# Residual codec kernel: output stores issued by ScalarE's queue, loads alone on SyncE's, and all queues ordered anew

## The chip, the core and the metric

The kernel runs on one core of a Trainium2 chip. The metric is device time in microseconds. Times before come from three runs (615.65, 626.93 and 618.35 us); one further execution was profiled.

## The reference

A sequence x of 2 x 16000 rows of 512 channels (bfloat16) is filtered along time with three taps per channel, put through SiLU, quantized by four residual stages of eight code vectors each, and the sum of the chosen vectors is filtered with three taps again:

```python
for i in range(K):                      # K = 3
    z = z + xp[:, i:i+T, :] * dw_enc[i][None, None, :]
z = _silu(z)
res = z
for s in range(Nq):                     # Nq = 4, eight vectors in each codebook
    cb = codebooks[s]
    d2 = |res|^2 - 2.0 * res @ cb.T + |cb|^2
    idx = d2.argmin(-1)
    sel = cb[idx]
    q = q + sel
    res = res - sel
for i in range(K):
    y = y + qp[:, i:i+T, :] * dw_dec[i][None, None, :]
```

(The line of d2 is shortened; xp and qp are z's input and q padded by one row at both ends.)

## The kernel before

The rows are cut into 18 tiles. A tile has G groups of 128 rows; 14 tiles have G = 16, and the first and last two have 6 and 8. Partition p of a tile holds the G consecutive rows that begin at its row G*p, and neighbouring tiles overlap by two rows, for the filters.

The steps of one tile, with the lines that the profile names:

- **Load.** G transposing DMAs from SyncE, one a group (L557), and one each for the rows before and behind (L565, L571), write the channels onto partitions in XT. There are two XT buffers.
- **Taps, SiLU.** For each half of the channels: three multiplications on VectorE or ScalarE (L599, L598), two sums on VectorE (L386), the exponential on ScalarE (L604), plus one (L606 or L605), the reciprocal on ScalarE (L616), the product on VectorE (L386, ZB). The exponential and the reciprocal need different tables, which ScalarE loads in between (1.28 us each).
- **Decide.** Products of ZB with itself and the codebooks on TensorE (L635), evacuated by VectorE (L669, L670); three stages of small VectorE instructions choose a vector and set a one-hot row; TensorE and a copy (OT, L716 on ScalarE or L717 on VectorE) turn it round for the next stage's correction. POOL copies one-hot rows (L704, L707).
- **Residual.** TensorE subtracts the chosen vectors from ZB in PSUM (L793, L798), eight evacuations a tile write ZB back (L820 on ScalarE or L821 on VectorE), and a fourth decision follows (L836 to L846).
- **Back.** TensorE applies the decoder to windows of one-hot rows (L762, then L870); each product of 1024 columns is cast from PSUM into half of a YB buffer, on ScalarE (L879) or VectorE (L880). There are four YB buffers of four groups each.
- **Store.** When both halves of a YB are written, SyncE issues its store (L902), from the same queue as the loads. The rows that overlap with a neighbouring tile are left out, and a store is cut so that most of it covers a multiple of 16 partitions. So one step issues one to three transfers: 128 partitions at once, or 112, 15 and 1. There are 64 such steps and 130 transfers.

All steps are entered into a list with their dependences and a planned duration, and a planner (class Plan, L17 to L182) hands out the order. Two strings of constants fix it: RANK, a rank for each step, by which each engine's queue is sorted; and WHERE, one letter for each step that can run on either of two engines (A for ScalarE, D for VectorE). The planned durations matter at one place: the planner lays the queues out in time, emits the instructions of all engines in the order of their planned starts, and puts filler products on TensorE (L922) where it expects TensorE to wait for over 1 us. Each engine then executes its own instructions strictly in that order. Transfers take turns on eight completion lanes in the order in which they are emitted, whichever engine issues them, and each waits until the previous one on its lane has landed.

In the store step before, the planned duration is 0.5 us on SyncE ("SP") with a tail of 4.0 us until the data has landed; a load is planned at 1.36 us (1.56 us in the first two tiles) with a tail of 1.5 us.

Of the kernel before, what the change touches and what calls it, by code (L numbers as in the profile page):

```python
# [12 lines left out]
ACT = mybir.ActivationFunctionType  # L13
# [172 lines left out]
def kernel(  # L186
# [32 lines left out]
    RANK = ("000102010102060500040d0h050a0d0V00090E010d0q0u070v0a0j0c0p030t0f0B020j0e0f0g0i0l0m0n0r0306080b0k0o0p0q03040e00050a06080c"  # L219
            "04060b05070103090d020h0p0z0n0m07070C0D0L0M0P0R0U0j0q0t040v0g0z0h0f15171l13161c040g0i0Z1f1g0b080900080605090x0A0F0G0c0J0K"  # L220
            "0O0W0f0g0i0r0h0l0i020n0H0o0S0y0N0s0k0l10190e0m0r0w0c0T0e0Y0a0I0b0Q0k110j0X120o14180u1k1d0s1a1b1e1h1i1j0w1r0y1t0A1w0k0l1A"
            "1B1C1D1E1F1G0s0m1J0n1K1L1M1N1O1P1Q1R1S1T0t0o1V0p1W1X1Y1Z202122230u0q250r0s0I270t0v0K0L0w0y0Q0M0z0A0P0O0C0D2o2r2t2x2D0F0V"
            "0J2S0K0X1A0N2Y1d09080d0e0b0c070f030a1o1m1n0x1p1s1q1u0C0E0B1x1v1y1z1H0D1I0F1U0G240H260u0x2b2e2f2g2h2i2j0v0B2m0E2k2p2s2y2u"
            "2z2B2C2E2F0w0G0U0H2G2H2I2L2M2N2O2P0x0I2R0L0M0Y0Z0O0P11140Q0R13120S0T15160U0V37383a3c3d0Y1a121l131n1P111c141h1q0w0m0k0x0g"
            "0u0j0l0h0v0s0i0r0q0p0t0n0o292a0J282c0N2d2l0S2Q2n2q2v0R2w0T2A2K0W2T103117390W0X3g0Z103j3l3n3q3s3v3x0y151f163z3C3D3F3B3E3H"
            "3I3J3K0z171j183M3O3Q3P3R3S3T3U0C1b1m1d1e1q1p1g1h1s1t1i1j1v1u1k1l1x1y1o1p4q1r1t4K4O4P4R4T1H1O1N1S1P1Y271O1R1Q1U251M1T1X1X"
            "2h1V1W1W202c0M0A0I0P0O0C0K0D0G0y0L0z0H0F0B0E0N0J2X2W2U2V2Z303233191b351834363b3e3f3i1d3t1e3N1g3L191c3Z1a1f41454447494b4d"
            "0A1m4f1n4i4l4o4r4j4m4s4t4u4v0B1q4z1s4w4x4y4B4C4E4F4G0G1u1C1w1x1E1G1z1C1I1J1D1E1K1L1F1G1M1N1J1K5e1S1U5t5v5x5y5B1Y5H262327"
            "252m252222242l2j2j2p2l2s2i2g2r2n2w1513110W120V0Y0R0X0Q0S0T170Z0U1014163m3o3k3p3r3u3w3y1k3Y1i3G3A3V3W1o3X401w4k1z4A1A4D1v"
            "1y4S1A1B4U4W4V4X4Z502J520D1I1P1L555a5c5f5d5g5h5j5k5m0E1R5r1T5o5p5q5u5w5z5A5C0K205K2829282b2a2b272a2d2f2d2e2g2h2f2h2l2q6t"  # L230
# [29 lines left out]
    WHERE = ("ADDADADADDDADDDDDDDDADAAAAAAADADDDDADDAADDDDADDADAAAAAAAAAAAAADDADADDDDDAADDAAAAAAAAAAAAAAAAAAAADDDDDDADADDDDDDDAAAAAAAA"  # L260
            "ADAAAAAAAADDDDDDDADDDADDADDAAAAAAAADAAADAAAADDDADDDDDDDADDADDDAAAAAAAAAAAAAAAADDADDDDDDDDDDDDADAAAAAAAADAAAAAAAADDDDDDDD"
            "DDDDDDAADAADAAAAAAAAAAAAAADDDDDDDDADDADDDAAAADAAADAAAAAAAAAADDDDDDDDDDDDDDAADAAAAAADAAAAAAAAAADDDDDDDDDDDDDDDDDDAAAAAAAA"
            "AAAAAAAADDDADDDDDDDDDDDDDADAAAAAAAAAAAAAAADDDDDDDDDDDDADAAAAAAADAAADAAAAAAAADDADDDDDDDDDDDDDDAAAADAAADAAADAAAADDDDDDDDDD"
            "DDDDADDADAAAAAAAAAAAAAADDDDDDDDDDDDDDDADDADAAADDADAAAADDAADDDDDDDDDDDDDDADDAAAAAAADDAAADDDDDDDADADDDDDDDAAADDADADDAAD")
# [286 lines left out]
    def load(st):  # L551
# [6 lines left out]
        for g in range(G):  # L558
            add("SP", 1.56 if n < 2 else 1.36, ("load", n, 0.01 * g), lambda g=g: one(g), [], [("X", n % NX, g + 1)], tail=1.5)
# [3 lines left out]
        if t0 and n:  # L563
            before = xf[r0 - 1:r0 - 1 + G * P, :].rearrange("(p g) d -> g p d", g=G)[0]
            add("SP", 1.56 if n < 2 else 1.36, ("load", n, 0.01 * G), lambda: nc.sync.dma_start_transpose(out=X[:, :, 0, :], in_=before), [], xe, tail=1.5)  # L565
# [286 lines left out]
    def back(st):  # L852
        n, GH = st["n"], st["GH"]
        W = OHW[n % NW]
        for k0 in range(0, GH, 2):
# [5 lines left out]
            for k in ks:  # L861
# [98 lines left out]
```

## Time and profile before

| What | us |
|---|---|
| Median of three runs (lowest, highest) | 618.35 (615.65, 626.93) |
| The profiled execution, whole time | 618.01 |
| The profiled execution, its span | 616.2 |
| TensorE busy | 512.9 |
| POOL busy | 57.3 |

The span reaches from the first to the last instruction of the profiled execution. SPq and ACTq are the DMA issues of SyncE and ScalarE; the profile doesn't count them as busy time of an engine. The granted clock of TensorE was 0.971 of full speed on the mean. The DMA engines moved 72.1 MB at a mean of 117 GB/s, and the transfers of SyncE's queue took 54.0% of the sixteen DMA engines' time.

### The profile page before, as it was taken

What the parts mean: (1) busy time and instruction counts of PE and PEld (TensorE: products, weight loads), DVE (VectorE), ACT (ScalarE), POOL (GpSimd) and SP (SyncE); (2) the same over time, 40 slices, a digit from 0 to 9 for tenths busy, and PEclk for the clock granted to TensorE, in tenths of its full rate; (3) what the DMA queues carried; (4) which work ended last, traced back from release to release, by engine and by line L of the source; (5) the groups of instructions that cost most, each with busy time, mean ns of one, the idle gap of its engine ahead of it and who ended that gap; (6) DMA issues with size and microseconds to landing.
All of it is one profiled execution on the core that took longest, in us unless ns stands there. A gap on an engine that the chain in (4) does not pass through costs nothing.

```text
span 616.2 us, 27776 instructions
## 1 busy us (share of the span) xinstructions
PE 512.9 (83%) x12628; PEld 241.8 (39%) x12628; DVE 557.3 (90%) x1110; ACT 548.9 (89%) x432; POOL 57.3 (9%) x93
## 2 busy tenths in 40 slices
PE   4979879788967777888877888869987889989994
PEld 1435334244434233343442343433344244434542
DVE  6887998999999999999998999979999999997653
ACT  2895889989999999999988999879998999999764
POOL 3000000301010010202010000100012011110000
PEclk9898979999998999999997999989999999999998
DMA  5455555556558935575665657566664734602336
GB/s 114 82 99 92 100 88 88 111 114 115 103 97 140 172 80 122 87 168 121 115 171 74 171 114 166 105 121 140 131 129 84 171 99 103 157 4 105 107 118 203
DMA packets 163981, 72.10 MB, mean 117 GB/s; under 512 B 155568, under 2 KB 155600, under 8 KB 163863
## 3 DMA queue, kind: packets, MB, share of 16 engines
q1 hardware_dynamic: 163646, 69.90, 54.0%
q8 instruction: 98, 1.61, 1.1%
q10 hardware_dynamic: 216, 0.43, 0.3%
q14 instruction: 21, 0.16, 0.2%
HBM read 0.43 MB, written 32.77 MB: 54 GB/s over the span
## 4 chain that ended last, share of the span: by engine, by line
ACT 29%; DVE 28%; PE 13%; SPq 12%; issue 11%; DMA 6%; DVEq 0%; ACTq 0%
SPq L557 10%; ACT YB L879 7%; DVE ZB L386 7%; ACT ZB L820 6%; ACT EX L616 5%; ACT EX L604 5%; DMA XT<-in_x_dram 4%; DVE TB L599 4%; DVE TA L386 3%; PE banks L870 3%; PE banks L793 3%; PE banks L635 3%; DVE EX L606 2%; DVE TA L599 2%; PE banks L798 2%
## 5 line engine op out<-in xcount | busy, mean ns | idle before, releaser
L879 ACT CAST YB<-banks 128x1024 bf16<-128x1024 f32 x117 | 113.6, 1029 | 14.0 <-DMA out_dram<-YB 4.5
L820 ACT CAST ZB<-banks 128x1024 bf16<-128x1024 f32 (+2 forms) x125 | 108.9, 926 | 14.6 <-PE banks L798 14.3
L604 ACT ACTIVATE EX<-ZB 128x4096 bf16<-128x4096 bf16 (+2 forms) x36 | 115.1, 3196 | 5.3 <-DVE ZB L386 5.2
L922 PE MATMUL banks<-MSK,IDENT 128*128 128x512 bf16 x465 | 115.1, 389 | 2.3 <-DVE S L670 0.7
L616 ACT ACTIVATE EX<-EX 128x4096 bf16<-128x4096 bf16 (+2 forms) x36 | 115.0, 3199 | 0.2
L635 PE MATMUL banks<-ZB 128*32 128x64 bf16 x8064 | 92.0, 198 | 5.7 <-issue 3.0
L635 PEld LDWEIGHTS <-ZB 128*32 128x32 bf16 x8064 | 77.1, 96 | 48.9 <-issue 43.6
L599 DVE TENSOR_SCALAR TB<-XT,WENC 128x2048 bf16<-128x2048 bf16 (+2 forms) x128 | 86.8, 689 | 7.3 <-DMA XT<-in_x_dram 3.6
L870 PE MATMUL banks<-WDEC,OHW 128*128 128x512 bf16 x252 | 75.3, 389 | 21.6 <-ACT YB L879 11.4
L798 PE MATMUL banks<-OHR,WR 32*128 32x512 bf16 (+2 forms) x1152 | 82.0, 357 | 0.9 <-ACT OHR L750 0.8
L707 POOL COPY OHD<-OHA 128x256 bf16<-128x256 bf16 (+2 forms) x36 | 36.3, 1007 | 461.8 <-DVE OHA L386 461.8
L386 DVE TENSOR_TENSOR TA<-TA,TB 128x4096 bf16<-128x4096 bf16 (+2 forms) x36 | 72.7, 2018 | 4.8 <-ACT TB L598 3.7
L386 DVE TENSOR_TENSOR ZB<-ZB,EX 128x4096 bf16<-128x4096 bf16 (+2 forms) x36 | 73.2, 2036 | 2.9 <-ACT EX L616 2.9
L386 DVE TENSOR_TENSOR ZB<-TA,TB 128x4096 bf16<-128x4096 bf16 (+2 forms) x36 | 72.9, 2026 | 0.9 <-ACT TB L598 0.8
L793 PE MATMUL banks<-ZB,IDENT 64*64 64x512 bf16 (+2 forms) x576 | 55.0, 370 | 13.2 <-ACT YB L879 3.6
L922 PEld LDWEIGHTS <-IDENT 128*128 128x128 bf16 x465 | 42.5, 99 | 50.6 <-issue 8.4
L793 PE MATMUL banks<-ZB,UP 64*64 64x512 bf16 (+2 forms) x576 | 52.9, 354 | 0.0
L599 DVE TENSOR_SCALAR TA<-XT,WENC 128x2048 bf16<-128x2048 bf16 (+2 forms) x65 | 44.6, 695 | 5.5 <-DMA XT<-in_x_dram 4.4
L798 PEld LDWEIGHTS <-WR 32*128 32x128 bf16 x1152 | 23.7, 93 | 59.4 <-issue 51.2
L793 PE MATMUL banks<-ZB,DOWN 64*64 64x512 bf16 (+2 forms) x576 | 41.9, 367 | 0.0
L870 PEld LDWEIGHTS <-OHW 128*128 128x128 bf16 x252 | 20.7, 98 | 45.2 <-issue 25.2
L606 DVE TENSOR_SCALAR EX<-EX 128x4096 bf16<-128x4096 bf16 (+2 forms) x33 | 36.7, 1112 | 1.3 <-ACT EX L604 1.3
(129 smaller groups left out, 566.8 us busy)
## 6 DMA issues: line engine op xcount, KB each, us to landing
out_dram<-YB SPq DMA_DIRECT2D x33, 448.0 KB
out_dram<-YB SPq DMA_DIRECT2D x28, 512.0 KB
XT<-in_x_dram SPq DMA_TRANSPOSE x283
out_dram<-YB SPq DMA_DIRECT2D x30, 60.0 KB
out_dram<-YB SPq DMA_DIRECT2D x31, 2.0 KB
out_dram<-YB SPq DMA_DIRECT2D x2, 224.0 KB
YB<-in_dw_dec_dram ACTq DMA_DIRECT2D x1, 384.0 KB
out_dram<-YB SPq DMA_DIRECT2D x1, 384.0 KB
```

Source lines behind the costliest of these rows:

```text
L386: add("DVE", cost, key, lambda: nc.vector.tensor_tensor(out=out, in0=a, in1=b, op=op), reads, writes, **kw)
L557: nc.sync.dma_start_transpose(out=X[:, :, g + 1, :], in_=src[g])
L599: lambda dst=dst, src=src, w=w: nc.vector.tensor_scalar(out=dst, in0=src, scalar1=w, scalar2=None, op0=ALU.mult),
L604: add("ACT", act(2 * R), ("exp", n, h), lambda: nc.scalar.activation(v(ex), Z, ACT.Exp, scale=-1.0), zt, [("EX", sl), "ACTTAB"], hold="E")
L616: nc.scalar.add_instruction(mybir.InstActivation(name=nc.get_next_instruction_name(), engine=mybir.EngineType.Activation, func=ACT.Reciprocal,
L635: nc.tensor.matmul(o[HB * q:HB * (q + 1), u * ZW:(u + 1) * ZW].rearrange("p (s c) -> p s c", s=2), lhsT=blk, rhs=both, start=False, stop=( ...
L793: nc.tensor.matmul(at(r)[to], lhsT=dia[h, h], rhs=Z[h, i, r:G:RG, :], start=start, stop=False)
L798: nc.tensor.matmul(at(r), lhsT=WR[v][g, i * P:(i + 1) * P], rhs=W[g, v // 3, 0:rows_of[r], :], start=False, stop=stop)
L820: either({"ACT": act_psum(2 * k * P), "DVE": dve(2 * k * P)}, key(1), lambda dst=dst, src=src: nc.scalar.copy(dst, src()), lambda dst=dst, ...
L870: nc.tensor.matmul(o, lhsT=W[:, k, PADC:PADC + P], rhs=WDEC[u], start=True, stop=not wrap)
L879: either({"ACT": act_psum(1024), "DVE": dve(1024)}, key, lambda dst=dst, box=box: nc.scalar.copy(dst, ps(box)), lambda dst=dst, box=box: n ...
L922: nc.tensor.matmul(PS[j // 2][:, 512 * (j % 2):512 * (j % 2) + NMK * ZW], lhsT=IDENT, rhs=MSK.rearrange("p u w -> p (u w)"), start=True, s ...
```

## The change

The store step is entered for ScalarE in place of SyncE, and its transfers are issued by ScalarE's queue. Its planned duration is now 0.06 us and 0.1 us for each of its transfers; the cutting of the store into transfers (pieces) is taken out of the old function, unchanged, to count them. Loads stay on SyncE, planned at 1.4 in place of 1.36 us. RANK and WHERE are both replaced as a whole, so every queue has a new order, and some steps change between ScalarE and VectorE. Nothing else differs: the steps, their sizes and their number are the same.

```diff
-    RANK = ("000102010102060500040d0h050a0d0V00090E010d0q0u070v0a0j0c0p030t0f0B020j0e0f0g0i0l0m0n0r0306080b0k0o0p0q03040e00050a06080c"
...
+    RANK = ("00010200040706000203090b060d0b0P02070o0i0s0608010r0y0J0c0v0h0F0w0z0i0s050c0h0k0l0m0o0p0307080f0g0j0n0u00050k05030d01040h"
...
-    WHERE = ("ADDADADADDDADDDDDDDDADAAAAAAAADADDDDADDAADDDDADDADAAAAAAAAAAAAADDADADDDDDAADDAAAAAAAAAAAAAAAAAAAADDDDDDADADDDDDDDAAAAAAAA"
...
+    WHERE = ("DAADDDDDADADDDDAAADDAAAAAAAAADADADDDDDAADDDDDDDDDAAAAAAAAAAAAADDADADDDDADDADDAAAAAAAAAAAAAAADAAAADDDDDDADADDDDDDDAAAAAAA"
...
         for g in range(G):
-            add("SP", 1.56 if n < 2 else 1.36, ("load", n, 0.01 * g), lambda g=g: one(g), [], [("X", n % NX, g + 1)], tail=1.5)
+            add("SP", 1.56 if n < 2 else 1.4, ("load", n, 0.01 * g), lambda g=g: one(g), [], [("X", n % NX, g + 1)], tail=1.5)
...
-            add("SP", 0.5, ("back", n, ks[-1] / GH), lambda Y=Y, g0=2 * k0, g1=2 * (ks[-1] + 1): store(st, Y, g0, g1), [("Y", y)], [],
+            parts = pieces(st, 2 * k0, 2 * (ks[-1] + 1))
+            add("ACT", 0.06 + 0.1 * len(parts), ("back", n, ks[-1] / GH), lambda Y=Y, g0=2 * k0, parts=parts: store(st, Y, g0, parts), [("Y", y)], [],
                 tail=4.0)
 
-    def store(st, Y, g0, g1):
-        r0, a, e, G = st["row0"], st["a"], st["e"], st["G"]
-        view = outf[r0:r0 + G * P, :].rearrange("(p g) d -> p g d", g=G)
+    def pieces(st, g0, g1):
+        a, e, G = st["a"], st["e"], st["G"]
         runs = []
...
-        for p0, p1, lo, hi in split:
-            nc.sync.dma_start(out=view[p0:p1, lo:hi, :], in_=Y[p0:p1, lo - g0:hi - g0, :])
+        return split
+
+    def store(st, Y, g0, parts):
+        r0, G = st["row0"], st["G"]
+        view = outf[r0:r0 + G * P, :].rearrange("(p g) d -> p g d", g=G)
+        for p0, p1, lo, hi in parts:
+            nc.scalar.dma_start(out=view[p0:p1, lo:hi, :], in_=Y[p0:p1, lo - g0:hi - g0, :])
```

The two loads of the neighbouring rows (L565, L571) change as L559 does.

More of the change, by code (lines that the diff above doesn't have):

```diff
@@ L260 @@
[L260 to L264, printed above, removed]
+    RANK = ("00010200040706000203090b060d0b0P02070o0i0s0608010r0y0J0c0v0h0F0w0z0i0s050c0h0k0l0m0o0p0307080f0g0j0n0u00050k05030d01040h"
+            "030708040a0206090c0c0b0o0C0p0l01060t0B0K0L0N0R0X0i0i0u0a0v0d050h0j14161l111b1c0p0e0e0Y121f0b08090g0q0l04040a0C0G0H0e0O0Q"
+            "0S0T0f0f0j0n0e02000f0m0M0A0D0j0I0903190g0m0k0u0n0x0d0U0g0Z070E0a0W0V10151317180q1a0s1n0r1e1g1d1h1i0t1j0w0y0z1v0A1x0k0l1B"
+            "1D1C1E1F1G1H0q0m0F0n1I1J1L1N1M1O1P1Q1R1S0r0o1X0p1T1U1V1Y1Z2021220t0q240r0s0K0J0u0w0N0M0x0y0S0O0z0A0R0Q0C0D2p2s2u2w2x0F0W"
+            "0J2R0L0Y110N2X150f0c0a080e09010d0b050x1o1k1m1p1q1r1s0D0E0B1t1u1w1y1z1A1K0G1W0H230I250t0v292b2c2e2f2g2h0v0B2k0E2i2j2t2v2o"
+            "2r2z2B2D2E0w0G2H0H2G2J2L2K2M2N2O2P0x0I2Q0K0M0Z100O0P17130Q0R14160S0T19180U0V3638393a3c0Y1d121j151o1r101g131l1w0o0r0v0j0u"
+            "0p0x0l0q0n0t0k0s0g0w0i0m0h27280L262a0P2d2l0U2F2q0T2n2m2y0V2C2I0X2S122Z1a370W0X3e0Z113i3k3j3m3p3r3t0y141i163x3B3D3E3z3C3F"
+            "3G3I3J0z171n183L3O3Q3P3R3S3T3U0C1b1q1d1e1u1t1f1h1x1y1i1j1z1D1k1l1C1B1o1p4u1s1t4L4O4Q4S4T1H1S1K1W1Q1Y211N1X1O5s241P1V1X23"
+            "261T201W22290H0A0E0J0F0L0B0G0N0O0M0y0I0P0C0z0K0D2V2T2U2W2Y3130321c1e351b33343b3f3d3g1f3u1h3M1k3K191c3X1a1g40444346484a4c"
+            "0A1m4k1n4e4h4j4l4n4p4q4r4s4t0B1q4x1r4v4w4z4A4B4C4D4F0D1v4H1w1x1I1M1z1A1L1N1D1E1Q1P1F1G1R1T1L1M5i1R1U5t5v5x5z5B1Y5F282b22"
+            "2c2h2528272a2j2k2q2m2r2u2i2p2j2t2w170Z0U100R0W0Q0X0V16120T1514110Y130S3q3n3l3o3s3w3v3y1p3Y1m3H3N3A3V1s3W3Z1A4g1E4y1F4E1u"
+            "1y4M1B1C4V4Y4X4Z50512A530E1I571J55595d5f5a5c5g5h5j5l0F1S5r1V5o5q5u5w5y5A5C5E0L205K26292e5Z2a2b2f2i2c2f2l2m2g2h2n2o2l2r6w"
+            "2s2t6D6H6I6K6M2B6O2E2E2I2G2I2D2D2F6T2L2J2H2M2J2Q2O2M2Q2N2P1c1l1n1d1b1j18191m1o1e1a1f1k1g1h1p1i4142451v47494b4d1G4J4o4i4m"
+            "4f4G1H4I4K1J4U1U5m1Z5D21235L1Z245O5S5Q5V5W5X3h610G2d2g2e6365696b686c6e6f6h6j0J2o6l2p6m6n6q6s6t6v6y6A0P2u6C2v2w6J2y2x2z2A"
+            "2B2C2R7k2O2S2T2U2S2W2X7D33357I7K7P7R7T39343c383j3e3m3b373e393b3f3a3g3c3k3i3d3n3i3p1x1G1D1y1u1w1E1v1q1A1r1C1F1z1t1s1H1B4P"
+            "4R1K4N4W521O54255M565b585e5k5p5n5G275T2d642k6g2n2q6x2y2A6Q6W6V6X6Z70710M2K742P7375777b797c7e7g7i7l0O2U2T2V7o7q7s7r7t7u7v"
+            "7w0Q2Y7y2Z302Z2Y32363132373833353m3o3g3h3s3v8t3y3A8G8K8N8Q8S3F8W3L3x3K3z3C3P3A3R3E3J3Q3B3T3D3G3M3y3S3I3L1M1L1N1V1Z1U1W1Y"
+            "1P1X1I1Q1J1S1T1O1K1R5J5N5I5H5P5U5R5Y2s6z676066626a6i6d6k2v6G2x6L2z6R2G2H6Y2L2N767h7d7j7z7B7E0R312X347G7M7O7Q7J7N7S7U7W7Y"
+            "0S3a363d80838584878b8d8e0T3p8i3r3t3l3q3u3w8A3o3B3C3s3t3D3E3v3u3H3I913N3O95999d9i9k443S483W4c40424d3Y4i414d493V4g3Z4e4F4i"
+            "4H4l4m2g28292e2a2c23252421272b2f2022262d0H0I6o6u6p6r6B6F6E6N2F7a6U2C6S6P722K787f2V7A2W7H30813h3k883l3q8j8n8m8o8q8r8u0U3x"
+            "8y3z8x8z8B8D8C8E8H8J8M8R0V3G8Y3J8T8V8X909296989b0W3V3F3X3Y3K3M3Z409n3O41423Q3P43469w3U4a4b9G4e4j9T9W9Ya0a24m444q464pak4c"
+            "4J4o4N4q4t4M4p4Q4v4z4P4s4W4w4R2u2m2x2i2k2t2l2s2n2o2q2w2p2v2r2j0K0N2h2R7n7m7p7x7F7C7L3f8l7Z7X827V868a898c3j8v3n8F3r8Z3U3W"
+            "9e45479v9B9z9D9F9H9I0X4f9K4h9L9P9S9V9O9U9X9Za1a30Y4na54oa6a8aaa9abacaeaf104sah4u4v48494w4x4b4a4y4z4f4k4A4Bay4h4L4OaO4S4U"
+            "b3b5b7b9bb4Y4x5b4I5c4J4U5j4N5o4Q4W5p4S5r4V4X5y515x53552P2D2L2E2A2z2N2G2M2y2I2C2K2F2O2H2J2B8g8h8f8k8p8s8w8I3w948O8U8P8L93"
+            "9a979c3N9t3R9A3T9E4k4lad4r4tajapalaratavax0Z4D4j4IaBaDaEaGaFaHaJaLaNaP114RaT4TaUaXaZaYb1b2b4b6144Vbd4Z51bq4B52534A4C5557"
+            "4E4G58594H4F5d5fbL5q5sc0c2c4c6c85C545H575F595b5P5d5T5g5i5M5a5N5c5f5R5e5S5h5j302V372T2U2W31342R2X2Y353236332Q2Z2S9g9f9h3H"
+            "9j9m9l9o3X9N9p9q9s9r9u9x9y9C43ag45an47as4C4Eaz4G4KaIaVaQb0b8babc124Xbf50bebgbibkbjblbmbnbobp1354bs56bvbybzbxbBbCbEbG165a"
+            "bJ5e5g4LbO5h5i4O4M5k5l4TbT5t5u4Z4Y5z5Bck5A5EcqctcvcycA5J585V5k6a5x5I695y6i5A5H685w6f5C5M665u6e5B5N3p3m3k3g3o3l393h3j3c3e"
+            "3i3f3n383a3b3d9M9Q9J9Ra4a7aiam4gaCaqauawaoaAaK4naM4rbh4ybH4DbQ5m5nbV5v5wc7c9cacccfchcj155Dcm5GclcncpcscrcucwcxczcB175KcE"
+            "5OcDcFcHcKcMcOcQcR1b5W5l5X5Y5n5o5Z605rd661635q5t6567dl5v6b6cdr6h6kdEdIdKdMdP6qdT6y5R6z5T5X6A5S6K5Y646E5U6N5Z616G5V6I6062"
+            "3C3y3w3s3x3u3B3A3r3F3D3t3H3z3G3v3q3EaRaS4uaWbrbtbubw4KbXbIbDbFbAbKbNbMbP4PbZ50ce52co5I5LcG5Q5UcTcVcWcYd0d2d41862d764d8da"
+            "dddgdcdfdidkdmdo196ddq6gdsdudwdvdxdydzdA1c6jdC6l6m5F5E6n6o5K5G6u6ve85O6w6x5P5Q6B6Dej6H6MezeCeEeFeG6PeJ6Y6a7a6j6m736f7d6o"
+            "6w766h7e6k6t7y6z7A6A6B3V3J403Q3M3I3K3R3X3L3Y3S3N3U3O3T3P3WbRbWbUbSbYc1c3c556cUcicgcdcbcCcJcIcL5md55pdh5zdB6p6rdU6s6te0e2"
+            "e3e5e7e9eb1e6Cef6Fedegeielekemeneoepeq1f6Jes6LetevexeweyeAeBeD1g6OeH6Q6ReReL6S6TeS676X706c6d71726g6e7c7gfD7l7rfWg1g2g4g5"
+            "7x6y7E6C7Lgu6I7Cgi7Fgk6F7I6D7T6K6N7Ogw7V6L6S4c4a4541424e48444g494f474h464d3Z4b43cNcPcScXcZd1d3d95DdRdb5sdjdedndtdpdD5JdZ"
+            "5Lee5WeI6U6WeT6V6ZeXf0eZf1f2f4f61h74fb75f8fafdfffefgfhfifjfk1i79fm7bfnfpfrfsftfufvfw1j7ffB7i7kfP6p7m7o6sfS7q7s6u6v7u7v6x"
+            "g77B7Ggm7M7SgCgDgEgHgJ7ZgL82gN886U6W836Q8agQ6X8bgR8g70728e6Z8i73744q4j4s4l4i4m4o4p4n4kdJdGdFdHdLdNdOdQ63eQdWdSdXdYe1e6e4"
+            "ea65eW68eY6bf77778flfofqfxfyfzdVfA1k7h6l7jfCfFfHfIfEfGfKfLfMfN1l7nfR7pfQfXfYfUfZg0g3g61o7zgc7J7K6G6E7P7Rgz6J7U7W6O6M7Y80"
+            "gM6P8c8dgSgTgUgVgW8jgY8n768o77798m758q787a4y4v4t4x4u4w4r1a1deuehecereKeNeMeP6ifJ6966eUeVf3f9f5fc6nfO6qfT6rfV7t7wg8gag9gb"
+            "gdgeeOgf1m7Dgj7Hggghglgogngpgqgrgsgt1n7N6H7QgvgxgAgygBgFgGgI1p7XgK81846RgO8586gP6T87896V6Y8f8h71gX8k8lgZh0h1h2h38ph48rh5"
+            "8s7b7c8th67d")
@@ new lines @@
+    WHERE = ("DAADDDDDADADDDDAAADDAAAAAAAAADADADDDDDAADDDDDDDDDAAAAAAAAAAAAADDADADDDADDADDAAAAAAAAAAAAAAADAAAADDDDDDADADDDDDDDDAAAAAAA"
+            "ADAAAAAAAADDDDDDDADDDADDDDDADAAAAAADAAADAAAADDDADDDDDDDADDADDDAAADAAAAAAAAAAAADDADDADDDDDDDDDADAAAAAAAADAAAAAAAADDDDDDDD"
+            "DDDDDDAADAADAAAAAAAAAAAAAADDDDDDDDADDADDDDAAADAAADAAADAAAAAAADDDDDDDDDDDDDDDDAAAAAADAAAAAAAAAADDDDDDDDDDDDDDADDDAAAAAAAA"
+            "AAAAAAAADDDADDDDDDDDDDDDDADAAADAAAAAAAAAAADDDDDDDDDDDDADDDAAAADAADADAAAAAAAADDADDDDDDDDDDDDDDAAAADAAADAAAAAAAADDDDDDDDDD"
+            "DDDDDDDDDDAAAAAAADDDAADADDDDDDDDADDDDDDDDDAADAAADDDAADDAAADDDDDDDDDDDDDDADDAADAAADADAAAADDDDDDDAADDDDDDADADDAAAADDDAD")
@@ L564, in load @@
             before = xf[r0 - 1:r0 - 1 + G * P, :].rearrange("(p g) d -> g p d", g=G)[0]
-            add("SP", 1.56 if n < 2 else 1.36, ("load", n, 0.01 * G), lambda: nc.sync.dma_start_transpose(out=X[:, :, 0, :], in_=before), [], xe, tail=1.5)
+            add("SP", 1.56 if n < 2 else 1.4, ("load", n, 0.01 * G), lambda: nc.sync.dma_start_transpose(out=X[:, :, 0, :], in_=before), [], xe, tail=1.5)
         else:
@@ L570, in load @@
             behind = xf[r0 + 1:r0 + 1 + G * P, :].rearrange("(p g) d -> g p d", g=G)[G - 1]
-            add("SP", 1.56 if n < 2 else 1.36, ("load", n, 0.01 * G), lambda: nc.sync.dma_start_transpose(out=X[:, :, G + 1, :], in_=behind), [], xo, tail=1.5)
+            add("SP", 1.56 if n < 2 else 1.4, ("load", n, 0.01 * G), lambda: nc.sync.dma_start_transpose(out=X[:, :, G + 1, :], in_=behind), [], xo, tail=1.5)
         else:
```

40 lines of the change are left out of this document (removed).

## The prediction

> **What bounds the kernel now.** I read the page first: busy shares and the chain of waits.
>
> ```profile
> span 616.2 us, 27776 instructions
> PE 512.9 (83%) x12628; PEld 241.8 (39%) x12628; DVE 557.3 (90%) x1110; ACT 548.9 (89%) x432; POOL 57.3 (9%) x93
> ACT 29%; DVE 28%; PE 13%; SPq 12%; issue 11%; DMA 6%; DVEq 0%; ACTq 0%
> ```
>
> Two engines, VectorE and ScalarE, are each busy nine tenths of the span, and the chain that ended last goes through both about equally. SyncE's queue carries a further 12% of that chain, so I asked next in which stage the two engines are idle. The table of stages has, after its length, PE, PEld, DVE, ACT and POOL busy.
>
> ```profile
> 0.00:80.00 80.00, 63.73 (x815) 29.84 (x816) 65.41 (x186) 56.46 (x66) 9.22 (x39) 0.96 0.50 96
> 80.00:560.00 480.00, 401.30 (x10474) 189.18 (x10473) 460.93 (x834) 456.00 (x326) 46.84 (x49) 0.98 0.58 119
> 560.00:617.00 57.00, 47.89 (x1343) 22.82 (x1339) 30.98 (x92) 36.45 (x42) 1.24 (x5) 0.94 0.37 126
> 320.00:340.00 20.00, 14.64 (x306) 5.93 (x307) 17.02 (x30) 15.77 (x14) 1.43 (x1) 0.83 0.58 105
> ```
>
> In the body (80 to 560 us) VectorE idles 480 - 460.9 = 19.1 us and ScalarE 24.0 us: at most 4 to 5% of it can be won without taking work away. The filling (0 to 80) and the draining stage (from 560) hold the larger gaps. The list of waits tells what a late transfer costs, and SyncE's own list why it is late (total, times, longest, us):
>
> ```profile
> ACT TB L598 <- DMA XT<-in_x_dram: 8.6, 3, 5.3
> ACT TB L598 <- DMA XT<-in_x_dram: 2.4, 1, 2.4
> ACT YB L879 <- DMA out_dram<-YB: 4.5, 2, 4.0
> DVE TA L599 <- DMA XT<-in_x_dram: 4.4, 1, 4.4
> DVE TA L599 <- DMA out_dram<-YB: 0.9, 1, 0.9
> SPq L902 <- ACT YB L879: 96.2, 19, 17.5
> ```
>
> The second row is the same wait within 0 to 80 us, so ScalarE loses 8.6 - 2.4 + 4.5 = 10.7 us to transfers in the body, VectorE 4.4 + 0.9. SyncE stands 96.2 us at stores whose YB is not yet written, with the loads queued behind. The timeline shows both ways in which this hurts:
>
> ```profile
> 318.62 1.74 SPq L557 DMA_TRANSPOSE XT<-in_x_dram  x1
> 320.40 1.27 SPq L902 DMA_DIRECT2D out_dram<-YB  x3
> 326.04 2.84 ACT L879 CAST YB<-banks 128x1024 bf16<-128x1024 f32 x3 [4.02 <-DMA out_dram<-YB]
> 392.41 5.03 SPq L557 DMA_TRANSPOSE XT<-in_x_dram  x3
> 397.54 2.26 SPq L902 DMA_DIRECT2D out_dram<-YB  x3
> 399.84 4.43 SPq L557 DMA_TRANSPOSE XT<-in_x_dram  x3
> 404.07 2.00 ACT L598 ACTIVATE TB<-XT,WENC 128x2048 bf16<-128x2048 bf16 x1 [5.26 <-DMA XT<-in_x_dram]
> ```
>
> At 320 a store came late behind transposes, and ScalarE had no free YB for 4.0 us. Near 398 it is the other way round: loads went out behind a store, and ScalarE's taps waited 5.3 us for them.
>
> **Part 1: SyncE loses the stores.**
>
> ```profile
> XT<-in_x_dram SPq DMA_TRANSPOSE x283
> 0.74 3.92 SPq L557 DMA_TRANSPOSE XT<-in_x_dram  x3
> L902 SPq DMA_DIRECT2D out_dram<-YB x130: 227/428/2394, 109.1 to 612.0; - x130
> ```
>
> A load costs SyncE 3.92 / 3 = 1.31 us, all of them 283 x 1.31 = 371 us. Stores add 130 x 0.43 = 56 us and the 96 us of waiting, together 523 us, and loads end near 528 us: the queue is full until then. Without stores it has some 150 us of slack, so the late loads and late stores of the body go: 10.7 us on ScalarE. On VectorE 4.4 + 0.9 us go, and the 20.0 - 17.0 = 3.0 us that it idled in the stage 320 to 340 behind the missing YB: 8.3 us. What is late next is what fills the rest of the idle time, products of TensorE and the other engine's halves. The first store went out at 109 us, so nothing is won in the filling stage. A load still waits for the transfer that used its completion lane eight transfers earlier, which may now be a store of ScalarE; those are old by then, and I cost this at nothing unless ScalarE runs behind.
>
> **Part 2: ScalarE issues 130 stores.** The trace has three DMA issues by ScalarE, at the start:
>
> ```profile
> 0.73 1.28 ACT L273 ACT_TABLE_LOAD   x1 [0.73 <-PEq L944]
> 0.76 0.60 ACTq L367 DMA_DIRECT2D WER<-in_dw_enc_dram  x1
> 1.40 0.36 ACTq L368 DMA_DIRECT2D CB<-in_codebooks_dram  x1
> 4.25 0.36 ACTq L371 DMA_DIRECT2D YB<-in_dw_dec_dram  x1
> ```
>
> Two of them ran beside the table load that stood ahead of them. So an issue hides under the instruction in progress, while whatever stands behind it cannot start. In the order of the changed kernel the 130 issues form 53 unbroken runs on ScalarE (18 of one, 5 of two, 21 of three, 9 of four to six). From each run's issue time I took the duration of the instruction just ahead of it, or nothing where that instruction is the cast being stored. At 0.36 us an issue (the rows above) 20 us stay uncovered, at 0.43 us (SyncE's median) 27; 9 to 11 of these lie in the last sixty instructions, where ScalarE has gaps. The body keeps 11 to 16 us; I take 14. Bounds: 0, if the sequencer runs several instructions ahead, and 130 x 0.43 + gaps = 61 us over the whole, if nothing hides. A gain is excluded, since SyncE's relief is counted above. Queued behind a waiting store are all of ScalarE's later casts and exponentials, and TensorE waits for the banks that they free.
>
> **Part 3: the queues found anew.** The same steps are dealt out differently. By the counts of the two orders ScalarE gives up 5 YB casts, 6 full ZB casts and 7 OT copies, and takes 3 taps of 2048; VectorE the reverse. The rows (shape, count, busy us, mean ns):
>
> ```profile
> L879 ACT CAST YB<-banks 128x1024 bf16<-128x1024 f32 x117 | 113.6, 1029 | 14.0 <-DMA out_dram<-YB 4.5 <-PE banks L870 4.5 <-PE banks L745 1.6
> L820 ACT CAST ZB<-banks 128x1024 bf16<-128x1024 f32 x99 | 95.7, 1024 | 5.7 <-PE banks L798 5.5
> L598 ACT ACTIVATE TB<-XT,WENC 128x2048 bf16<-128x2048 bf16 x12 | 24.1, 2006 | 10.6 <-DMA XT<-in_x_dram 8.6 <-DVE ZB L386 1.4 <-DVE TA L386 0.6
> L716 ACT COPY OT<-banks 128x128 bf16<-128x128 bf16 x14 | 4.0, 284 | 1.4 <-PE banks L712 1.4
> L880 DVE CAST YB<-banks 128x1024 bf16<-128x1024 f32 x9 | 11.0, 1221 | 2.1 <-PE banks L874 1.3 <-PE banks L870 0.7
> L821 DVE CAST ZB<-banks 128x1024 bf16<-128x1024 f32 x13 | 15.8, 1217 | 0.6 <-PE banks L798 0.6
> L599 DVE TENSOR_SCALAR TB<-XT,WENC 128x2048 bf16<-128x2048 bf16 x100 | 74.7, 757 | 7.2 <-DMA XT<-in_x_dram 3.6 <-issue 2.6 <-DVE OHA L386 0.5
> L717 DVE COPY OT<-banks 128x128 bf16<-128x128 bf16 x14 | 3.0, 216 | 0.0
> ```
>
> ScalarE: -5 x 1.03 - 6 x 1.02 - 7 x 0.28 + 3 x 2.01 = -7.2 us. VectorE: +5 x 1.22 + 6 x 1.22 + 7 x 0.22 - 3 x 0.76 = +12.6 us. Groups that move one or two instructions are left out. TensorE gets the same products and 480 fillers instead of 465. Fillers stand where it is expected to wait, so nothing says that the new order holds fewer gaps. What a new order does to the remaining waits has no row: it could close the 10 to 13 us that stay in the body or open as many. I take 0.
>
> **Part 4: the end.**
>
> ```profile
> 607.99 1.23 DVE L880 CAST YB<-banks 128x1024 bf16<-128x1024 f32 x1 [0.50 <-PE banks L874]
> 589.32 23.72 SPq L902 DMA_DIRECT2D out_dram<-YB  x21
> ```
>
> The last cast ended at 609.2 us and SyncE's last issue at 613.0, 3.8 us later. Now four issues stand behind ScalarE's last cast, about 1.6 us and a wait for VectorE's casts: between 2 us won and none; I take 1.
>
> **The sum.** ScalarE's body: 456.0 - 7.2 + 14 + (24.0 - 10.7) = 476.1 us, 3.9 below the 480 of now. VectorE's body: 460.9 + 12.6 + (19.1 - 8.3) = 484.3, 4.3 above. VectorE is then the fuller engine, but its idle time shrinks where its partner keeps up; I go between the mean of the two (+0.2) and VectorE alone (+4.3): +2.1. With the end, 616.2 + 2.1 - 1.0 = 617.3 us of span. The profiled execution took 618.0 us for 616.2 of span, so 617.3 + 1.8 = **619 us**; the median before, 618.35, is that of this execution within 0.1%.
>
> **The rivals.**
>
> *Two queues, one descriptor generator (slower).* If an issue by ScalarE must let SyncE's transpose finish, it meets one 371 / 528 = 70% of the time and waits half of 1.27 us: 0.44 us more, 0.86 us an issue. My walk then leaves 47 us uncovered in the body: 456.0 - 7.2 + 47 + 13.3 = 509 us for ScalarE, 29 us over, about 647. It passes 2% from about 0.65 us an issue. For it: SyncE's own stores, at a median of 428 ns, reach 2394. Against it: the issue at 1.40 us took 0.36 us while three transposes ran without a break from 0.74 to 4.66. The Trainium skill (Perfetto Trace Analysis, section "DMA Instruction — HWDGE (DVE, Sync)") states that the descriptor generator is shared between the sequencers and locked for exclusive use, and that the wait for the lock is part of the profiled time; the 0.36 us row disagrees for that one, and no row shows it under load. Chance 0.2.
>
> *ScalarE waits in order for others.* A store now also waits on ScalarE's queue for VectorE's cast of the other half, and for the transfer eight earlier on its lane, mostly a load. If ten of the 64 store steps stand 1.5 us, the body grows by 15 us: 633. The order puts two or more other instructions between the last cast by ScalarE and the store in two thirds of the cases, which speaks against it. Chance 0.1.
>
> *The freed queue lets the new order close the gaps (faster).* If 4 us of idle time stay on VectorE instead of 10.8, issues hide wholly, and the draining stage, where VectorE works 31 of 57 us, shortens by 10: 484.3 - 6.8 = 477.5, so 618.0 - 2.5 - 10 with ScalarE below that: about 605. Against it: the fillers, and 5 us more work on the two engines together. Chance 0.2.
>
> **How the numbers follow.** The forecast, 619, keeps 0.5, with 608 to 630 as its own range (terms of +-14 on the uncovered issues, shared by two engines, and +-10 on the gaps). The range 602 to 640 takes in the faster case, the in-order waits and the lighter half of the shared generator; left out is the rest of that one and odd ends. By 2%, about what a measurement of this kernel can tell from no change, faster means below 606: 0.2 (three quarters of the faster case, and 0.05 from below the forecast's own range). Slower means above 630.7: 0.29 (the shared generator, most of the in-order waits, the forecast's upper end). Within: 0.51.
>
> **What would show it.** SyncE's queue has no waits for YB, and the two waits for DMA in the body are gone (part 1). DMA issues on ScalarE of 0.36 to 0.43 us, with ScalarE idle 10 to 20 us in all around them (part 2); a mean above 0.65 us is the shared generator. VectorE busy near 570 us and ScalarE near 541 (part 3). A span far off with all this right would lie in gaps of the new order.

## The result, and the profile after

The changed kernel takes 753.04 us (median of four runs, 750.11 to 758.71) where the kernel before took 617.00 beside it: 1.223 times as long, with an interval of 1.212 to 1.234. The forecast was 619 in a range of 602 to 640. The profiled execution has a span of 756.9 us. From its page come the span, the busy shares, the shares of the chain that ended last, and one line of the costliest groups:

```profile
span 756.9 us, 27660 instructions
PE 525.9 (69%) x12545; PEld 246.2 (33%) x12643; DVE 567.7 (75%) x1125; ACT 543.4 (72%) x417; POOL 62.0 (8%) x93
...
ACT 26%; DVE 21%; SPq 19%; PE 15%; issue 8%; DMA 7%; ACTq 3%; DVEq 0%
...
L793 PE MATMUL banks<-ZB,IDENT 64*64 64x512 bf16 (+2 forms) x576 | 58.2, 392 | 101.1 <-ACT ZB L820 57.6
```

VectorE and ScalarE are busy within about 2 us of what was forecast, and idle for longer: VectorE for 189 us of the span (59 before), ScalarE for 214 (67 before). SyncE's queue has risen from 12% of the chain to 19%, although it has lost 130 of its transfers. In the row shown, TensorE stands 57.6 us for evacuations by ScalarE. The table of stages (length, then PE, PEld, DVE, ACT, POOL busy, clock, DMA share, GB/s) tells where:

```profile
0.00:80.00 80.00, 62.36 (x800) 28.53 (x810) 66.29 (x187) 54.91 (x65) 8.47 (x39) 1.00 0.53 99
200.00:320.00 120.00, 72.95 (x1681) 31.95 (x1690) 87.50 (x147) 80.18 (x52) 14.35 (x11) 0.83 0.47 103
320.00:440.00 120.00, 74.03 (x1899) 32.88 (x1910) 80.67 (x137) 80.30 (x60) 11.11 (x7) 0.82 0.41 94
```

The filling stage is as before. In the two stages of the body that are shown, both engines idle for 27 to 33% of the time; in the others, up to 700 us, for 19 to 25%. So the loss is spread over the whole body. The granted clock of TensorE is lower there too (0.83 and 0.82, with TensorE busy for 61 and 62% of the time, against 1.00 at 78% in the filling stage); on the mean it is 0.885, and was 0.971 before. ScalarE's list of waits (total us, times, longest) names what it stands for:

```profile
ACT TB L598 <- DMA XT<-in_x_dram: 23.0, 2, 12.3
ACT YB L879 <- DMA XT<-in_x_dram: 19.1, 3, 9.9
ACT L616 <- DMA XT<-in_x_dram: 17.3, 2, 13.4
ACT ZB L820 <- DMA out_dram<-YB: 16.9, 2, 11.9
ACT TA L598 <- DMA XT<-in_x_dram: 16.6, 1, 16.6
ACT YB L879 <- DMA out_dram<-YB: 13.7, 2, 10.7
ACT ZB L820 <- DMA XT<-in_x_dram: 12.4, 3, 8.2
ACT EX L604 <- DMA XT<-in_x_dram: 11.2, 1, 11.2
...
ACT L604 <- DMA XT<-in_x_dram: 5.0, 1, 5.0
...
ACT L604 <- issue: 2.8, 1, 2.8
ACT YB L879 <- issue: 2.8, 1, 2.8
...
ACT L616 <- DMA out_dram<-YB: 2.5, 1, 2.5
...
ACT L604 <- DMA out_dram<-YB: 0.7, 1, 0.7
```

The eleven rows with a DMA add up to 138.4 us in 19 stretches; before, transfers held ScalarE for 10.7 us in the body. The five rows with XT that aren't taps (L598) can't be what they seem. A cast of a product from PSUM (L879, L820), a load of the table for the reciprocal (L616) and the exponentials (L604) read nothing that a load writes: XT is read by the taps alone. The wait belongs to something that stands ahead of them in ScalarE's queue. The timeline shows it at one of the longest places, first ScalarE's rows, then SyncE's, then VectorE's:

```profile
306.12 2.00 ACT L598 ACTIVATE TB<-XT,WENC 128x2048 bf16<-128x2048 bf16 x1
...
309.82 1.03 ACT L820 CAST ZB<-banks 128x1024 bf16<-128x1024 f32 x1
316.14 11.23 ACTq L907 DMA_DIRECT2D out_dram<-YB  x4
327.47 2.00 ACT L598 ACTIVATE TA<-XT,WENC 128x2048 bf16<-128x2048 bf16 x1 [16.62 <-DMA XT<-in_x_dram]
```

```profile
258.83 26.24 SPq L557 DMA_TRANSPOSE XT<-in_x_dram  x16
...
308.15 3.81 SPq L557 DMA_TRANSPOSE XT<-in_x_dram  x3
312.06 1.21 SPq L571 DMA_TRANSPOSE XT<-in_x_dram  x1
313.31 9.49 SPq L557 DMA_TRANSPOSE XT<-in_x_dram  x7
```

```profile
331.50 0.29 DVE L690 TENSOR_TENSOR PR<-banks,S 128x128 bf16<-128x128 f32 x1 [15.77 <-ACT ZB L820]
```

ScalarE's cast ends at 310.85. Four stores come next in its queue; the first goes out at 316.14, the fourth by 327.37, and only then does the tap behind them start. In the same stretch SyncE works through a run of loads. That run had stood still from 285.07 to 308.15: the tap on ScalarE at 306.12 ended at 308.12, and the loads went on 0.03 us later. VectorE stands 15.77 us beside ScalarE. So a store waits for a load, the load has waited for a tap, and the tap stood on an engine that earlier stores had held up. Taps on both engines held that load: one on VectorE ran until 306.84, beside the one on ScalarE. SyncE's own list puts most of such waits down to VectorE's taps (total us, times, longest):

```profile
SPq L557 <- DVE TB L599: 132.7, 8, 25.2
```

Why a store should wait for a load is read from the compiled programs. Loads by SyncE and stores by ScalarE take turns on the same eight completion lanes, and each transfer waits until the one eight places ahead of it has landed, which is enforced by a wait in the queue of the engine that issues it. In the changed kernel 75 of the 130 stores wait in this way for a load; the other 55 follow a store. One statement in the section on the kernel before needs a correction: the places are handed out in the order of a timeline of all queues that the framework works out for itself at compile time, not simply in the order of emission. The first store is the 58th transfer that the kernel emits, and has the 74th place.

The trace shows these waits store by store, since it records each transfer's semaphore, one for each lane. In the changed kernel ScalarE has 27 gaps of over 0.6 us just ahead of a store, 128.1 us in all. At 26 of them (127.4 us) the lane was last used by a load, and the store goes out within 0.1 us of that load's last completion. The store at 316.14 is one: the load before it on its lane was issued at 313.32 and had landed at 316.06. The rows with XT above hold only 104.6 us, so most of the wait in the rows that name out_dram is of the same kind.

The issue itself is short, as the group of the stores shows (duration in ns, minimum, median and maximum, and the first and last start):

```profile
L907 ACTq DMA_DIRECT2D out_dram<-YB x130: 233/355/2177, 90.1 to 752.8; - x130
```

The wait isn't in that duration: it is time before the issue, in which the profile shows ScalarE idle and nothing of its queue. The Trainium skill (Perfetto Trace Analysis, section "DMA Instruction — HWDGE (DVE, Sync)") says so: what the profiler reports of such an instruction begins after its wait for semaphores. The trace agrees: ScalarE idles from 310.85 to 316.14, and the issue that follows is no longer than others:

```profile
316.14 0.34 ACTq L907 DMA_DIRECT2D out_dram<-YB  x1
```

### The profile page after: what moved, and what is told of

Same layout as the page of the kernel before. It is cut to its first block, busy times and chain, and to the rows that moved or that the text cites. A ratio compares the mean times of both kernels' runs of the same rounds, so it can differ in the third digit from the quotient of the medians.

```text
span 756.9 us, 27660 instructions
## 1 busy us (share of the span) xinstructions
PE 525.9 (69%) x12545; PEld 246.2 (33%) x12643; DVE 567.7 (75%) x1125; ACT 543.4 (72%) x417; POOL 62.0 (8%) x93
## 4 chain that ended last, share of the span: by engine, by line
ACT 26%; DVE 21%; SPq 19%; PE 15%; issue 8%; DMA 7%; ACTq 3%; DVEq 0%
SPq L557 17%; ACT EX L616 6%; DVE ZB L386 6%; DMA XT<-in_x_dram 5%; ACT EX L604 5%; ACT YB L879 5%; ACT ZB L820 4%; PE banks L793 4%; PE banks L927 4%; DVE TA L386 3%; DVE TB L599 3%; ACTq L907 3%; PE banks L798 3%; PE banks L635 2%; ACT TB L598 2%
## 5 line engine op out<-in xcount | busy, mean ns | idle before, releaser
L820 ACT CAST ZB<-banks 128x1024 bf16<-128x1024 f32 (+2 forms) x120 | 103.8, 912 | 55.4 <-PE banks L798 23.8
L879 ACT CAST YB<-banks 128x1024 bf16<-128x1024 f32 x112 | 108.6, 1032 | 42.8 <-DMA XT<-in_x_dram 19.1
L604 ACT ACTIVATE EX<-ZB 128x4096 bf16<-128x4096 bf16 (+2 forms) x36 | 114.8, 3193 | 22.5 <-DMA XT<-in_x_dram 11.2
L793 PE MATMUL banks<-ZB,IDENT 64*64 64x512 bf16 (+2 forms) x576 | 58.2, 392 | 101.1 <-ACT ZB L820 57.6
L616 ACT ACTIVATE EX<-EX 128x4096 bf16<-128x4096 bf16 (+2 forms) x36 | 114.7, 3196 | 0.2
L870 PE MATMUL banks<-WDEC,OHW 128*128 128x512 bf16 x208 | 69.5, 400 | 41.0 <-ACT YB L879 21.3
L707 POOL COPY OHD<-OHA 128x256 bf16<-128x256 bf16 (+2 forms) x36 | 41.7, 1158 | 582.9 <-DVE OHA L386 568.8
L798 PE MATMUL banks<-OHR,WR 32*128 32x512 bf16 (+2 forms) x1152 | 88.9, 383 | 0.2 <-DVE OHR L750 0.2
L793 PEld LDWEIGHTS <-IDENT 64*64 64x64 bf16 x576 | 21.6, 107 | 129.6 <-issue 123.6
L793 PE MATMUL banks<-ZB,UP 64*64 64x512 bf16 (+2 forms) x576 | 56.8, 376 | 0.0
L793 PE MATMUL banks<-ZB,DOWN 64*64 64x512 bf16 (+2 forms) x576 | 45.7, 395 | 0.0
L598 ACT ACTIVATE TB<-XT,WENC 128x2048 bf16<-128x2048 bf16 (+1 forms) x14 | 25.9, 1850 | 27.2 <-DMA XT<-in_x_dram 23.0
```

The lines of the kernel that those rows point to most:

```text
L604: add("ACT", act(2 * R), ("exp", n, h), lambda: nc.scalar.activation(v(ex), Z, ACT.Exp, scale=-1.0), zt, [("EX", sl), "ACTTAB"], hold="E")
L616: nc.scalar.add_instruction(mybir.InstActivation(name=nc.get_next_instruction_name(), engine=mybir.EngineType.Activation, func=ACT.Reciprocal,
L793: nc.tensor.matmul(at(r)[to], lhsT=dia[h, h], rhs=Z[h, i, r:G:RG, :], start=start, stop=False)
L798: nc.tensor.matmul(at(r), lhsT=WR[v][g, i * P:(i + 1) * P], rhs=W[g, v // 3, 0:rows_of[r], :], start=False, stop=stop)
L820: either({"ACT": act_psum(2 * k * P), "DVE": dve(2 * k * P)}, key(1), lambda dst=dst, src=src: nc.scalar.copy(dst, src()), lambda dst=dst, ...
L870: nc.tensor.matmul(o, lhsT=W[:, k, PADC:PADC + P], rhs=WDEC[u], start=True, stop=not wrap)
```

## The experiments

The theory: stores in ScalarE's queue wait for loads on shared completion lanes. The rivals: the new order of all queues is bad; the issues themselves cost ScalarE the time (a shared generator among the reasons); SyncE's or the DMA engines' traffic.

**The new order with the queue of before.**

```diff
-            nc.scalar.dma_start(out=view[p0:p1, lo:hi, :], in_=Y[p0:p1, lo - g0:hi - g0, :])
+            nc.sync.dma_start(out=view[p0:p1, lo:hi, :], in_=Y[p0:p1, lo - g0:hi - g0, :])
```

> The changed kernel with its new order and planned durations, but the stores issued by SyncE's queue again. Theory (ScalarE stands at stores whose completion lane is still held by a load that has not landed; 138 us of ScalarE's idle time lie directly behind stores): without stores on ScalarE these waits go, 757 - 138 = 619 us, within 605 to 650 since SyncE now waits at stores again. Rival (the new order itself is bad): stays above 720 us. Rival (issuing costs ScalarE much): 757 less 130 issues of 0.36 us and what follows from them, 700 us or more.

Measured: 615.28 us against 618.56 before, a ratio of 0.9961 (0.9931 to 0.9991). Its page's busy shares and, from the lists of waits, ScalarE's only wait for a transfer and SyncE's longest:

```profile
PE 520.0 (85%) x12643; PEld 242.8 (40%) x12643; DVE 564.9 (92%) x1125; ACT 542.9 (89%) x417; POOL 67.4 (11%) x93
```

```profile
ACT YB L879 <- DMA out_dram<-YB: 2.5, 1, 2.5
SPq L907 <- ACT YB L879: 82.1, 19, 20.3
```

The busy times are those of the changed kernel (ScalarE 542.9 and 543.4, VectorE 564.9 and 567.7), and one word in one line takes 138 us away. The order isn't the cause. SyncE still waits 82.1 us for casts, but 76.2 us of it lie behind its last load, which ends at 501.8; only 5.9 us hold up loads, where it was 45.5 us in the kernel before.

**The old order with the new queue.** The reverse edit on the kernel before:

```diff
-            nc.sync.dma_start(out=view[p0:p1, lo:hi, :], in_=Y[p0:p1, lo - g0:hi - g0, :])
+            nc.scalar.dma_start(out=view[p0:p1, lo:hi, :], in_=Y[p0:p1, lo - g0:hi - g0, :])
```

> The kernel before with its old order, only the stores issued by ScalarE's queue. Theory (lane waits on ScalarE's queue): above 680 us, with ScalarE idle for DMA behind stores by over 60 us in all. Rival (the new order is what is bad): 610 to 635 us, with the issues' uncovered time alone added. Rival (issues cost): 618 + 14 to 61 us of issues, 632 to 680.

Measured: 736.56 us in one run, 118.0 above the kernel before. ScalarE's list has the same strange rows, of which these are the largest; with the smaller ones transfers hold it for 120.7 us:

```profile
ACT EX L604 <- DMA XT<-in_x_dram: 34.5, 3, 12.9
ACT ZB L820 <- DMA XT<-in_x_dram: 34.3, 4, 11.8
```

The old order was made for another queue and loses nearly as much. So the queue alone does it, in either order.

**The new order with POOL's queue.** POOL's transfers have completion lanes of their own in the compiled program.

```diff
-            nc.scalar.dma_start(out=view[p0:p1, lo:hi, :], in_=Y[p0:p1, lo - g0:hi - g0, :])
+            nc.gpsimd.dma_start(out=view[p0:p1, lo:hi, :], in_=Y[p0:p1, lo - g0:hi - g0, :])
```

> The changed kernel with its new order, the stores issued by POOL's queue, whose transfers use completion lanes of their own. Theory (loads and stores share eight lanes): no wait of ScalarE for a load behind a store, and no load behind a store: 605 to 650 us, where POOL's own copies (OHD, OHA) may run late behind a waiting store and cost part of it. Rival (the new order is bad): above 720 us.

Measured: 621.58 us in one run; transfers hold ScalarE for 1.1 us. Two queues at once for the same transfers lose none of the 138 us when the second is POOL's. This run changes more than the lanes, since the stores now stand on an engine that has little else to do (POOL is busy 142.8 us, with the 130 issues counted, against 67.4 in the run with SyncE's queue); by itself it can't single out the lanes. It isn't better than SyncE's queue either: no gain shows from taking the stores away from SyncE.

**Loads that needn't wait for taps.** If loads are late because XT comes free late, loads into a buffer that nobody reads should bring the time back. Loads of the later tiles write XT[1]; their taps read XT[0], so the values of these tiles are not the reference's.

```diff
-        X = XT[n % NX]
+        X = XT[n] if n < 2 else XT[1]
...
-        X, xs = XT[n % NX], n % NX
+        X, xs = XT[n] if n < 2 else XT[0], n % NX
...
+        nc.vector.memset(XT[0][:, :, SIZES[0][0] + 2:, :], 0.0)
```

> The changed kernel, stores on ScalarE as in it, but the loads of tiles three to eighteen write into the second XT buffer, which nobody reads any more, and the taps of these tiles read the first one, so their output is not the reference's. Loads then wait for no taps and run ahead of the stores. Theory (a store waits for a load eight transfers earlier, which in turn waits for the taps to free XT): ScalarE's 138 us of waits behind stores fall below 30 us and the time to 600 to 630 us, with all 130 issues still on ScalarE. Rival (the issues themselves, or the shared generator, under SyncE's load): the 130 issues meet 283 transposes at a denser rate than before, and the time stays above 700 us.

Measured: 865.22 us in one run. The expectation was missed by 235 us, in the other direction. ScalarE's timeline at the first store, and SyncE's rows there:

```profile
82.95 1.07 ACT L820 CAST ZB<-banks 128x512 bf16<-128x512 f32 x2
169.73 0.38 ACTq L907 DMA_DIRECT2D out_dram<-YB  x1
170.13 1.28 ACT L616 ACT_TABLE_LOAD   x1 [86.11 <-DMA XT<-in_x_dram]
```

```profile
164.25 1.26 SPq L571 DMA_TRANSPOSE XT<-in_x_dram  x1
165.56 28.33 SPq L557 DMA_TRANSPOSE XT<-in_x_dram  x21
```

With nothing to hold the loads back, the compile-time timeline puts many more of them ahead of the first store, which is the 129th transfer of the compiled program where it was the 74th; the kernel emits it as the 58th in both. So it waits for the 121st: three setup transfers and 118 loads. Counted over the timeline, SyncE's rows up to 164.25 are 116 loads, so the 118th is the second of the run from 165.56, issued by 165.56 + 2 x 28.33 / 21 = 168.3. The trace has its landing at 169.63, and the store goes out at 169.73. That is the lane's wait, counted to the transfer. It also corrects the theory in a detail: loads needn't be late through the taps. A store stands for any load that the lane order puts eight places ahead of it, and 30 such stores are enough here for 250.5 us of waits (75 made 138.4 in the changed kernel). It isn't the number of such stores that sets the loss, but how far SyncE is behind when ScalarE comes to them.

**No loads to wait for.** The loads of the tiles from the third on are left out, once with the stores on ScalarE and once on SyncE.

```diff
         def one(g):
-            nc.sync.dma_start_transpose(out=X[:, :, g + 1, :], in_=src[g])
+            if n < 2:
+                nc.sync.dma_start_transpose(out=X[:, :, g + 1, :], in_=src[g])
...
+        for b in range(2):
+            nc.vector.memset(XT[b][:, :, SIZES[0][b] + 2:, :], 0.0)
```

The two loads of the neighbouring rows are cut in the same way; the second kernel has nc.sync in the store as well.

> The changed kernel without the loads of the tiles from the third on (their taps read what lies in XT; two memsets fill the rest of XT at the start), stores on ScalarE as changed. Leaves out 267 of 283 loads, so no store but the first few can stand behind a load on its lane. Lane theory (a store on ScalarE waits for a load that stands eight transfers before it): 590 to 625 us, all of ScalarE's waits for transfers together under 12 us, and within 12 us of the kernel of the next run. Rival (issuing or the traffic of the stores themselves hold ScalarE, whatever the loads do): still 680 us or more, and 60 us or more above the next run.

> The same without the same loads, stores issued by SyncE. Both theories: 585 to 620 us; it is the base of the run before.

Measured: 616.12 and 604.61 us, one run each. ScalarE's only row with a DMA in the first, and the group of its stores:

```profile
ACT YB L880 <- DMA out_dram<-YB: 1.9, 1, 1.9
```

```profile
L908 ACTq DMA_DIRECT2D out_dram<-YB x130: 233/362/1408, 75.7 to 609.8; - x130
```

All 130 stores are still issued by ScalarE (the median issue is 362 ns), and the 138 us are gone. So neither the issues nor the stores' own traffic are the cause. What is left, 11.5 us between the two runs, is most likely the price of issuing on ScalarE: its idle time that ends in "issue" is 5.8 us in the first and 0.4 in the second. That is not shown beyond one run each.

**The same number of stores, behind loads or not.** ScalarE issues the stores of the last six tiles in one kernel, of five tiles from the middle in the other; POOL issues the rest. All loads are there.

```diff
-            nc.scalar.dma_start(out=view[p0:p1, lo:hi, :], in_=Y[p0:p1, lo - g0:hi - g0, :])
+            (nc.scalar if st["n"] >= 12 else nc.gpsimd).dma_start(out=view[p0:p1, lo:hi, :], in_=Y[p0:p1, lo - g0:hi - g0, :])
```

The second has `5 <= st["n"] <= 9` for the condition.

> The changed kernel, all loads back; the stores of the last six tiles (42 transfers, 8 of which follow a load on their lane) are issued by ScalarE, the other 88 by POOL. Lane theory: 615 to 635 us, ScalarE's waits for transfers under 15 us. Rival (each store on ScalarE's queue costs about 1 us, (753 - 621) / 130, wherever it stands): 42 x 1.0 more than 621.6 us, about 664.

> As the run before, but it is the stores of tiles 5 to 9 that ScalarE issues (39 transfers, 34 of which follow a load on their lane); the other 91 are POOL's. Lane theory: the loss goes by the stores that follow a load, 34 of the 75 of the changed kernel, so 621.6 + 132 x 34 / 75, about 680 us, from 650 to 690, with 25 to 70 us of waits for XT's transfers on ScalarE. Rival (every store on ScalarE's queue costs the same): about 661 us, and the same as the run before within 10 us.

Measured: 622.89 and 687.92 us, one run each. The rows of ScalarE's list with a DMA, the last tiles' kernel first; of the other kernel's, the three largest:

```profile
ACT L604 <- DMA out_dram<-YB: 2.7, 1, 2.7
ACT YB L879 <- DMA out_dram<-YB: 2.7, 1, 2.7
```

```profile
ACT TB L598 <- DMA XT<-in_x_dram: 23.7, 2, 12.4
ACT ZB L820 <- DMA XT<-in_x_dram: 13.6, 3, 8.8
ACT YB L879 <- DMA XT<-in_x_dram: 11.9, 2, 10.5
```

42 stores at the end cost 1.3 us over the kernel with POOL's queue alone, 39 in the middle 66.3. A fixed price for each store is ruled out. All runs together, with the stores that wait for a load's lane counted from the semaphores of the transfers, and ScalarE's waits for transfers added up from its list:

| Kernel | Stores on ScalarE | of these behind a load | ScalarE's waits for transfers, us | Time, us |
|---|---|---|---|---|
| new order, stores on SyncE | 0 | 0 | 2.5 | 615.3 |
| new order, stores on POOL | 0 | 0 | 1.1 | 621.6 |
| without later loads, stores on ScalarE | 130 | 8 (early loads) | 1.9 | 616.1 |
| last six tiles | 42 | 8 | 5.4 | 622.9 |
| five middle tiles | 39 | 34 | 59.7 | 687.9 |
| old order, stores on ScalarE | 130 | 74 | 120.7 | 736.6 |
| the changed kernel | 130 | 75 | 138.4 | 753.0 |
| loads free of taps | 130 | 30 | 250.5 | 865.2 |

The waits are the loss, nearly: in the changed kernel 138.4 us of them against 753.0 - 615.3 = 137.7 us, in the last row 250.5 against 249.9, in the old order 120.7 against 118.0, and with the five middle tiles, the loosest fit, 59.7 against 66.3. Lanes for each queue alone, with all loads and all stores in place, were not tried, since the framework hands them out; POOL's queue is the nearest to that.

## Why the prediction was wrong

**What bounds, and Part 3, held.** VectorE was forecast at 557.3 + 12.6 = 569.9 us and is at 567.7, ScalarE at 548.9 - 7.2 = 541.7 and is at 543.4. What the new order is worth in its gaps was costed at 0 within 10 us; with the stores on SyncE it gains 3.3 us in all, the first experiment's 615.28 against 618.56. The faster rival (about 605) shows in neither of the kernels that have the new order without the lane waits (615.3 and 621.6).

**Part 1 failed, twice.** The step that cost the prediction is its last sentence: a transfer's wait for the one eight ahead on its lane was costed "at nothing unless ScalarE runs behind". It was looked at from the side of a load that waits for an old store. The other direction, a store on an in-order queue that waits for a load, was put among the rivals as "the transfer eight earlier on its lane, mostly a load", so the mechanism was known; its price was ten steps of 1.5 us, 15 us, and it measured 19 stretches of 7.3 us on the mean, 138.4 us. The 1.5 us had no row behind it. Two rows of the chain of waits before were against it (start and length, from a load's issue to its landing):

```profile
259.83 2.60 DMA XT<-in_x_dram
290.76 3.06 DMA XT<-in_x_dram
```

A store that comes just as its load is issued already stands about twice the 1.5 us, and at the 26 stores counted above the load took 2.7 to 6.0 us to land. On top of that comes the time until SyncE issues the load at all, and the lane order alone does not bound that: the whole wait was 16.6 us at 310.85, over four stores, and 86.1 us in the run with the free loads. The argument against that rival, that other instructions stand between the last cast and the store, gives VectorE time for its cast; it doesn't touch the lanes. Nor did the price hold the feedback: each stretch delays taps, and through them the next loads, as at 306 to 327 us.

The gain of Part 1 was not there either. It took 10.7 us on ScalarE and 8.3 us on VectorE from a SyncE without stores. With the new order and the stores still on SyncE, transfers hold ScalarE for 2.5 us; with SyncE free of them (POOL's queue) for 1.1 us, and the time isn't shorter. Those waits belonged to the old order, not to the queue. The sum for a full queue was misread as well: of the 96.2 us that SyncE stood at stores only 45.5 lie before the last load, and those are the ones that delay loads; in the new order 5.9 are left.

**Part 2 fits in its size, as far as single runs tell.** 14 us were forecast for the issues. The two runs without the later loads differ by 11.5 us. In the changed kernel the rows ended by "issue" hold 5.6 us in the list above; the other issues can't be told there from the waits for transfers.

**The shared generator** (647 us; a mean of the issues above 0.65 us) is not borne out: the mean over the 130 issues is 0.44 us and the median 355 ns, in a kernel where SyncE issues 283 transposes, and SyncE's own stores had a median of 428 before. The long ones are too few: 17 above 0.65 us, 2177 ns at most.

**Part 4** took 1 us off for the end, between 2 and none. The end of the changed kernel:

```profile
746.86 3.67 ACTq L907 DMA_DIRECT2D out_dram<-YB  x6
750.58 1.01 ACT L879 CAST YB<-banks 128x1024 bf16<-128x1024 f32 x1 [2.83 <-issue]
751.62 2.19 ACTq L907 DMA_DIRECT2D out_dram<-YB  x4
```

The last issue ends 2.2 us behind the last cast, 1.6 us less than the 3.8 before. But that cast had itself stood 2.83 us behind six issues, which Part 4 doesn't count. In a time that is 134 us off, neither matters.

**The chances.** The in-order rival had 0.1 and was priced just above the 2% line. With its real price the same order of events lies far outside the range. So the failure is one of size, and the chance leaned on that size.

## What to carry over

Before a transfer is moved to another engine's queue, ask what else that instruction waits for besides its data: where transfers of several queues share completion lanes, an engine that computes in order inherits the lateness of the other queue's transfers, and each wait holds all of its compute. Price such a wait by how far the other queue will be behind when the engine gets there, plus the time that the transfer takes to land, not by the issue's own duration. A row in which an instruction waits for data that it doesn't read is the sign of it: look at the DMA issue just ahead.

The fastest version that has all its loads is the new order with the stores left on SyncE: 615.28 us, 0.4% below the kernel before (0.1 to 0.7%). That is clear of the noise of these runs, but well within the 2% that the prediction counts as no change.

## What was not expected

- The Trainium skill (Perfetto Trace Analysis, section "DMA Optimizations") says that giving inputs to one issuing engine and outputs to another may make sense, above all where there are loops or control flow. Here the split cost 22% on ScalarE's queue (753.0 against 617.0 us) and won nothing on POOL's (621.6 in one run, against 615.3 with both on SyncE).
- Freeing the loads from the taps made the kernel slower, 865.2 us, because the places on the lanes are fixed at compile time: the first store moved from the 74th to the 129th place, behind loads that SyncE had still to issue.
- How long SyncE stands at stores says little by itself. In the fastest version with all loads it waits 82.1 us for casts, but 76.2 us of that have no load behind them.
